# Attention, soft mixture of experts and a dense layer pair in one kernel: a first round over half as many inner columns

## The chip, the core and the metric

The kernel runs on one core of a Trainium2 chip. The metric is the device time of one execution in microseconds (us); the median of three executions of the kernel before is 362.86 us (362.67 to 363.0). Engines are named as in the profile: PE is TensorE (matmul), PEld its weight loads, DVE is VectorE, ACT is ScalarE, POOL is GpSimd, SP is SyncE, which here only issues DMAs.

## The reference

Three parts, one feeding the next. 2304 tokens of width 512 come out of a windowed causal attention (4 batches, 8 heads, 576 positions, head size 64, window 64). A soft mixture of 8 experts with 4 slots each follows, and then the dense layers:

```python
scores = np.where(mask, scale * q @ k.T, -1e9)
x = softmax(scores) @ v                      # -> [2304, 512]
logits = x @ phi                             # 32 slots
slot_in = softmax(logits, axis=0).T @ x      # [32, 512]
slot_out[e] = np.maximum(slot_in[e] @ w1[e], 0) @ w2[e]   # 512 -> 1024 -> 512
x = softmax(logits, axis=1) @ slot_out       # combine, [2304, 512]
h = x @ w_in                                 # 512 -> 2048
out = (h * sigmoid(1.702 * h)) @ w_out       # 2048 -> 512
```

w_in and w_out arrive in float64; the kernel reads them as pairs of 32-bit words and narrows them to float32 itself.

## The kernel before

**Attention and routing.** 18 units of work (16 pairs of heads and two of left-over positions) go through a software pipeline; SP loads q, k and v of the units to come and, in the places given by `W_AT`, one or more blocks of the experts' weights of 1 MB each (`load_w`, 16 of w1 and 16 of w2). The first things that SP loads besides are five raw float64 blocks of 512 KB (`early_load`): four of w_in (128 rows each, inner columns 0 to 511) and one of w_out, into three slots of the weight pool (`raws`). Within the units `convert` narrows each of them over five units, in steps begun at the units in `CONV_AT`: one pass on ACT (L158), one on POOL (L161), three on DVE (L168, L172, L176).

**The experts.** `emit_w1` (L792) multiplies the 32 slots with w1, `emit_w2` (L834, then L893 and L901 for the last two blocks) with w2; four products run side by side on 32 columns of the array each. The w2 blocks come in the order in which they are used; the last one comes in three pieces. Behind the weights SP loads w_out blocks 1 to 4 and w_in blocks 4 and 5, still raw.

**Into the dense layers.** The combine with the slots and w_in are joined: M = slot_out @ w_in, 32 rows, is computed first, and h of a token is its 32 combine weights (`cT`) times M. The columns of M are made in pieces, `MCUT`. Piece 0 (128 columns) is made directly by `emit_m2(0)` (L943). The others go through `emit_m1` (L928, four products side by side, one for each 128 rows of w_in, then a copy to SBUF on ACT, L921) and `emit_m2` (L940, which adds the four up), with the rounded high part written by ACT (L948) and the low part by DVE (L951). Pieces 0 and 1 (columns 0 to 511) are made before the dense loop, the others within it.

**The dense loop.** `steps` is a list of 48 triples (group of inner blocks, round of 768 tokens, inner block of 128 columns). For each step `emit_h` makes h of the next step (L1014), ACT applies the gelu twice (L1002: once rounded, once whole) and DVE takes the difference (`emit_gl`, L1027); `emit_o` then adds the products with w_out's high and low part (L1046) for six tiles of 128 tokens, 18 matmuls in all, into six banks of PSUM, which are all of the accumulators there are. At the last inner block of a group the six are written to SBUF (L1069 on DVE, L1071 on ACT, for later groups an add on DVE, L1066). The order before is four groups of four blocks, and in each the three rounds. Between steps, lists written by hand say at which step a raw block of w_in (`more`) or w_out (`todo`) is narrowed (`conv_a` on ACT, L958; `conv_b` on DVE, four passes, L964, L168, L172, L176), when w_out is split in two (`out_w` on ACT, L982; `out_c` on DVE, L985), and when a further piece of M is made (`mid1`, `mid2`). Each engine takes its instructions in the order in which the program emits them. h, `emit_m1` and `emit_m2` in the loop share two PSUM banks.

Of the kernel before, what the change touches and what calls it, by code (L numbers as in the profile page):

```python
# [38 lines left out]

CONV_AT = {i: n for n, i in enumerate((3, 5, 7, 9, 11))}  # L40
W = (2, 1)
# [24 lines left out]

FP = 4

@with_exitstack
def attention_softmoe_ffn(  # L70
# [113 lines left out]
    def early_dst(n):  # L184
        return win_dst(n) if n < FP else wof[:, n - FP, :]

# [3 lines left out]
    def early_load(n):  # L190
        src = w_in[n] if n < FP else w_out[n - FP]
        if wide:
            raw_load(early_raw(n), src)
        else:
            nc.sync.dma_start(out=early_dst(n), in_=src)
# [397 lines left out]
    nc.sync.dma_start(out=phis, in_=phi.rearrange("p (k s) -> p k s", k=KD))  # L593
    raws = [wslot() for _ in range(3)]
    for n in range(2):
# [17 lines left out]
    for i in range(ns):  # L613
# [53 lines left out]
        if i < 2:  # L667
            for n in range(2 * i + 2, min(2 * i + 4, FP + N_WO)):
                early_load(n)
# [201 lines left out]
    def win_more():  # L871
        n = FP + len(iraw)
        if n == NF:
            return
        if n % FP == 0:
            winf.append(gp.tile([128, 4, 512], F32, tag="wi", name="wi", bufs=2))
        iraw[n] = gp.tile([128, 1024], F32, tag="iraw", name="iraw", bufs=2)
        if wide:
            raw_load(iraw[n], w_in[n])
        else:  # L880
            nc.sync.dma_start(out=win_dst(n), in_=w_in[n])
# [32 lines left out]

    MCUT = [0, 128, 512, 1024, 1536, DFF]
    msb = {}
    mcp = rawt[:, NE * 260:NE * 260 + 512]

# [5 lines left out]
    def emit_m1(j, tag, copy=True):  # L924
        a, w = MCUT[j], MCUT[j + 1] - MCUT[j]
        pm = bank(tag)[:, 0:w]
        for kk in range(KD):
            nc.tensor.matmul(  # L928
                pm[32 * kk:32 * kk + 32, :], soT[:, kk, 0:32],
                win_dst(4 * (a // 512) + kk)[:, a % 512:a % 512 + w],  # L930
                start=True, stop=True, tile_position=(0, 32 * kk))
        msb[j] = mcp[:, a % 512:a % 512 + w], pm
        if copy:
            m1_copy(j)

    def emit_m2(j, tag):
        a, w = MCUT[j], MCUT[j + 1] - MCUT[j]
        pm = bank(tag)[:, 0:w]
        if j:
            nc.tensor.matmul(pm, i4m, msb.pop(j), start=True, stop=True)  # L940
        else:
            for kk in range(KD):
                nc.tensor.matmul(  # L943
                    pm, soT[:, kk, :], win_dst(kk)[:, 0:w], start=(kk == 0), stop=(kk == KD - 1))
        o = mst[:, a:a + w]

        def hi():
            nc.scalar.copy(o, pm)  # L948

        def lo():  # L950
            nc.vector.tensor_tensor(  # L951
                out=o[64:128], in0=pm[64:128], in1=o[64:128].bitcast(F32), op=ALU.subtract)
        return hi, lo
# [37 lines left out]
    NR = NT // ROUND  # L991
    steps = [(p, r, FP * p + k) for p in range(NF // FP) for r in range(NR) for k in range(FP)]
    gs = {}
# [37 lines left out]
    def emit_o(n, between):  # L1031
        p, r, f = steps[n]
        first, last = f % FP == 0, f % FP == FP - 1
        g2 = gs.pop(n)
# [47 lines left out]
    for i in range(14):  # L1082
# [7 lines left out]
        if i == 6:  # L1090
            dctx.close()
            gp = ctx.enter_context(tc.tile_pool(name="gp", bufs=4))
            parts_for(0)
            for _ in range(4):
                wout_load()
            for _ in range(2):
                win_more()
        for f in ahead.get(i, ()):
            f()
# [23 lines left out]
    out_c(1)  # L1123
    out_a(2)
    out_b(2, (0, 1))


    todo = {}
    more, mid1, mid2 = {}, {}, {}
    for p, (at, bt, ms) in enumerate((  # L1130
# [3 lines left out]
        for k in range(FP):  # L1134
            more[at[k]] = FP * (p + 1) + k
            todo[bt[k]] = FP * (p + 1) + k
        mid1[ms[0]], mid2[ms[1]] = p + 2, p + 2
    low = None
    for n in range(len(steps)):
# [7 lines left out]
        if n in todo:  # L1147
            out_b(todo[n])
        if n == 1:
            out_b(3, (0, 1))  # L1150
        between = {}
        if n:
            emit_h(n + 1)
# [4 lines left out]
        if n in mid2:  # L1158
            def second():
                for f in emit_m2(mid2[n], "m"):  # L1160
                    f()
            between.setdefault(2, []).append(second)
        emit_o(n, between)
        if n < 2:
            out_b(n + 2, (2, 3))
        if n in todo or n < 2:
            low = todo.get(n, n + 2)
            out_w(low)
        if n == 0:
            out_a(3)  # L1170
        if n + 1 in more:
            conv_a(iraw[more[n + 1]], win_dst(more[n + 1]))
        if n + 1 in todo and n + 1 > 0 and todo[n + 1] not in wfs:
            out_a(todo[n + 1])
# [5 lines left out]
def _layout(q, k, v, moe_phi, moe_w1, moe_w2, moe2_w_in, moe2_w_out):  # L1180
# [25 lines left out]
    w2 = np.concatenate([w2[:15], last])  # L1206
    wi = moe2_w_in.reshape(4, 128, 4, 512).transpose(2, 0, 1, 3).reshape(16, 128, 512)
    wo = moe2_w_out.reshape(16, 128, 512)
    return {"qk": qk, "vt": vt, "sq": sq, "phi": ph, "w1": w1, "w2": w2,
# [25 lines left out]
```

## Time and profile before

| what | value |
|---|---|
| median of three executions | 362.86 us |
| the profiled execution | 362.31 us, its span 360.5 us |
| granted TensorE clock, mean | 1.000 |
| PE busy | 351.4 us (97%) |
| DVE, ACT busy | 240.5 us (67%), 195.6 us (54%) |
| DMA | 70.87 MB, mean 197 GB/s |

The span runs from the first to the last instruction of the program; 1.8 us of the execution lie around it. PE's 97% is over the whole span, in which DMA is at its limit for the first third and idle for most of the rest, so shares of the whole say little about one stage. Ends of matmuls are modelled.

### The profile page before, as it was taken

Reading aid. Unit: us, or ns where it says so; the run is one execution under the profiler, and the core shown is the slowest. Engines: PE = TensorE matmul, PEld = TensorE weight load, DVE = VectorE, ACT = ScalarE, POOL = GpSimd, SP = SyncE. Lnnn points to the kernel's source line nnn. Section 1 sums busy time; section 2 is a strip of 40 time slices with the busy share of each in tenths; the row PEclk is TensorE's granted clock in tenths of the full one; section 3 lists DMA queues with packets and bytes.
Section 4 is the critical chain, followed back from the end, with each engine's and each line's share of the span. In section 5 each row is a group of like instructions: output and inputs, shape, how many; then the busy total and the mean of one; then the engine's idle time right before and its main releaser. Section 6 shows DMA issues by size and latency. Waiting matters only on the chain.

```text
span 360.5 us, 7741 instructions
## 1 busy us (share of the span) xinstructions
PE 351.4 (97%) x3021; PEld 269.9 (75%) x3021; DVE 240.5 (67%) x527; ACT 195.6 (54%) x499; POOL 45.5 (13%) x90
## 2 busy tenths in 40 slices
PE   7999999998999999999999999999999999999995
PEld 6787787776634357888788887788886888888884
DVE  4666797976626228885867695988687876262624
ACT  2898899777314026765657444554455453333330
POOL 4366764630100000000000000000000000000000
PEclk9999999999999999999999999999999999999999
DMA  7999999999999994233131313140300000040404
GB/s 278 407 414 405 409 407 413 402 404 407 418 418 422 418 402 150 101 121 113 60 116 58 119 57 119 32 137 9 116 2 0 0 2 1 0 176 0 175 2 175
DMA packets 18180, 70.87 MB, mean 197 GB/s; under 512 B 2016, under 2 KB 2400, under 8 KB 14176
## 3 DMA queue, kind: packets, MB, share of 16 engines
q1 hardware_dynamic: 18000, 70.18, 50.3%
q8 instruction: 24, 0.39, 0.4%
q10 hardware_dynamic: 144, 0.20, 0.2%
q14 instruction: 12, 0.10, 0.1%
HBM read 65.65 MB, written 4.72 MB: 195 GB/s over the span
## 4 chain that ended last, share of the span: by engine, by line
PE 86%; DMA 9%; ACT 2%; issue 1%; DVE 1%; DVEq 0%; ACTq 0%
PE s L1046 18%; PE t L1046 18%; PE v L1046 18%; DMA w<-in_w_dram 8%; PE v L363 5%; PE m L1014 5%; PE m L348 5%; PE s L328 4%; PE s L313 2%; PE m L401 2%; ACT pa L340 2%; PE m L442 1%; PE m L492 1%; DMA rawt<-in_qk_dram 1%; PE m L928 1%
## 5 line engine op out<-in xcount | busy, mean ns | idle before, releaser
L1002 ACT ACTIVATE r<-m 128x384 fp32r<-128x384 f32 (+1 forms) x97 | 47.4, 491 | 80.6 <-PE m L1014 80.5
L1027 DVE TENSOR_TENSOR r<-g,r 128x384 fp32r<-128x384 f32 x96 | 51.4, 554 | 48.4 <-ACT g L1002 40.0
L1046 PE MATMUL t<-w,r 128*128 128x512 f32 x288 | 75.8, 395 | 0.0
L1046 PE MATMUL s<-w,r 128*128 128x512 f32 x288 | 74.3, 392 | 0.0
L1046 PE MATMUL v<-w,r 128*128 128x512 f32 (+2 forms) x291 | 73.4, 387 | 0.0
L1046 PEld LDWEIGHTS t<-w,r 128*128 128x128 f32 x288 | 53.8, 188 | 14.8 <-issue 4.0
L1046 PEld LDWEIGHTS v<-w,r 128*128 128x128 f32 x291 | 54.5, 188 | 11.3
L1046 PEld LDWEIGHTS s<-w,r 128*128 128x128 f32 x288 | 52.6, 188 | 8.5
L1002 ACT ACTIVATE g<-m 128x384 f32<-128x384 f32 x96 | 47.8, 499 | 0.0
L340 ACT ACTIVATE pa<-s,nm 128x128 f32<-128x128 f32 x140 | 41.0, 404 | 5.6 <-DVE nm L333 5.6
L333 DVE TENSOR_REDUCE nm<-s 128x4 f32<-128x512 f32 x35 | 22.5, 684 | 5.5 <-PE s L328 4.8
L1014 PE MATMUL m<-cT,w 128*128 128x384 f32 (+2 forms) x113 | 25.9, 320 | 0.0
L1014 PEld LDWEIGHTS m<-cT,w 128*128 128x128 f32 x113 | 20.8, 188 | 4.9 <-ACT g L1002 0.7
L348 PE MATMUL m<-ident,pa 128*128 128x128 f32 x144 | 20.9, 283 | 0.8 <-ACT pa L340 0.4
L348 PEld LDWEIGHTS m<-ident,pa 128*128 128x128 f32 x144 | 15.6, 140 | 5.0 <-PE s L328 1.7
L349 ACT COPY pa<-m 128x512 f32<-128x512 f32 x18 | 10.7, 596 | 10.2 <-PE m L348 10.2
L982 ACT CAST w<-wf 128x512 fp32r<-128x512 f32 x15 | 9.3, 623 | 9.3 <-DVE wf L176 9.3
L792 PE MATMUL s<-w,phis 128*32 128x512 f32 x128 | 14.1, 594 | 0.0
L382 DVE TENSOR_TENSOR arena<-v,rs 128x256 f32<-128x256 f32 x36 | 13.6, 420 | 0.6
L328 PE MATMUL s<-arena 64*64 64x128 f32 x352 | 13.8, 271 | 0.1
L985 DVE TENSOR_TENSOR w<-wf,w 128x512 fp32r<-128x512 f32 x15 | 10.3, 689 | 5.2 <-ACT w L982 4.9
L1066 DVE TENSOR_TENSOR w<-s,w 128x512 f32<-128x512 f32 x18 | 11.6, 684 | 2.8 <-PE s L1046 2.8
(218 smaller groups left out, 453.3 us busy)
## 6 DMA issues: line engine op xcount, KB each, us to landing
w<-in_w_dram SPq DMA_DIRECT2D x24, 1024.0 KB, 9.9
w<-in_w_out_dram SPq DMA_DIRECT2D x16, 512.0 KB, 3.4
arena<-in_w_dram SPq DMA_DIRECT2D x7, 1024.0 KB, 11.4
iraw<-in_w_in_dram SPq DMA_DIRECT2D x12, 512.0 KB, 3.3
arena<-in_qk_dram SPq DMA_DIRECT2D x10, 512.0 KB, 8.8
out_dram<-w SPq DMA_DIRECT2D x16, 256.0 KB, 2.1
arena<-in_vt_dram SPq DMA_DIRECT2D x13, 258.5 KB, 7.3
rawt<-in_qk_dram SPq DMA_DIRECT2D x6, 512.0 KB, 8.7
```

What stands on the lines that cost most here:

```text
L328: nc.tensor.matmul(st[h][rows[j], c, :], q, k, start=False, stop=(c == 3), tile_position=(64 * h, 64 * j))
L333: nc.vector.tensor_reduce(out=nm[:, h], in_=st[h], axis=AX.X, op=ALU.max, negate=True)
L340: nc.scalar.activation(out=pb[h][:, c, :], in_=st[h][:, c, :], func=ACTF.Exp, bias=nm[:, h, c:c + 1], scale=1.0)
L348: nc.tensor.transpose(tt[:, c, :], pb[h][:, c, :], ident)
L363: nc.tensor.matmul(pvt[i][h][64 * j:64 * j + 64, c, :], ab[h][:, c, 64 * j:64 * j + 64], v, start=True, stop=True, tile_position=(0, 64 * j))
L382: nc.vector.tensor_tensor(out=o, in0=pv[h][:, :, 1 - h:65 - h], in1=rs[:, h].unsqueeze(2).to_broadcast([128, 4, 64]), op=ALU.mult)
L792: nc.tensor.matmul(ph[32 * j:32 * j + 32, :], siT[:, kk, :], w1t[4 * r + kk][:, j, :], start=(kk == 0), stop=(kk == KD - 1), tile_position ...
L1002: nc.scalar.activation(out=(gh, g)[part][:, a:e], in_=ph[:, a:e], func=ACTF.Gelu_apprx_sigmoid)
L1014: nc.tensor.matmul(ph[:, c - a:e - a], mst[:, f * 128:f * 128 + 128], cT(c, e - c), start=True, stop=True)
L1027: nc.vector.tensor_tensor(out=gl, in0=g, in1=gh.bitcast(F32), op=ALU.subtract)
L1046: nc.tensor.matmul(accs[t][:, h], a[:, c], b[:, h], start=(first and k == 0), stop=(last and k == 2 and h.stop == 512))
L1066: nc.vector.tensor_tensor(out=o[:, h], in0=accs[t][:, h], in1=o[:, h], op=ALU.add)
```

## The change

Only two blocks of w_in are loaded early, and the host lays the first 512 columns out anew: blocks 0 and 1 now hold all 512 rows of columns 0 to 255, blocks 2 and 3 those of columns 256 to 511. Blocks 2 and 3 are loaded behind the experts' weights and behind w_out block 1, ahead of w_out 2 to 4, and are narrowed in steps 0 and 1 of the dense loop. Piece 1 of M shrinks from 384 to 128 columns; a new piece 2 (256 columns) is made within step 2. The first round of 768 tokens first goes through inner blocks 0 and 1 alone, and takes blocks 2 and 3 together with blocks 4 to 7 when the other two rounds have done blocks 0 to 3; so there are still 12 groups and 48 steps, and the first group ends at step 1, the next ones at steps 5 and 9 (before: 3, 7 and 11). w_out blocks 2 and 3 are narrowed for steps 4 and 5, w_in blocks 4 to 7 one step later than before. h of step 4 is emitted between the tiles of step 3.

```diff
-CONV_AT = {i: n for n, i in enumerate((3, 5, 7, 9, 11))}
+CONV_AT = {i: n for n, i in enumerate((3, 5, 7))}
 FP = 4
+E_IN = 2
     def early_dst(n):
-        return win_dst(n) if n < FP else wof[:, n - FP, :]
+        return win_dst(n) if n < E_IN else wof[:, n - E_IN, :]
     def early_load(n):
-        src = w_in[n] if n < FP else w_out[n - FP]
+        src = w_in[n] if n < E_IN else w_out[n - E_IN]
-    raws = [wslot() for _ in range(3)]
+    raws = [wslot() for _ in range(2)]
-            for n in range(2 * i + 2, min(2 * i + 4, FP + N_WO)):
+            for n in range(2 * i + 2, min(2 * i + 4, E_IN + N_WO)):
     def win_more():
-        n = FP + len(iraw)
+        n = E_IN + len(iraw)
-    MCUT = [0, 128, 512, 1024, 1536, DFF]
+    MCUT = [0, 128, 256, 512, 1024, 1536, DFF]
+    def win_of(a, w, kk):
+        if a < 512:
+            k = 256 * (kk % 2) + a % 256
+            return win_dst(2 * (a // 256) + kk // 2)[:, k:k + w]
+        return win_dst(4 * (a // 512) + kk)[:, a % 512:a % 512 + w]
     # emit_m1, emit_m2: win_of(a, w, kk) in place of win_dst(...)
-    steps = [(p, r, FP * p + k) for p in range(NF // FP) for r in range(NR) for k in range(FP)]
+    groups = [(r, range(0, FP if r else 2)) for r in range(NR)]
+    groups += [(r, range(FP * p + (0 if r or p > 1 else 2 - FP), FP * p + FP))
+               for p in range(1, NF // FP) for r in range(NR)]
+    steps = [(g, r, f) for g, (r, fs) in enumerate(groups) for f in fs]
     def emit_o(n, between):
-        p, r, f = steps[n]
-        first, last = f % FP == 0, f % FP == FP - 1
+        g, r, f = steps[n]
+        p = g // NR
+        first, last = f == groups[g][1][0], f == groups[g][1][-1]
     # behind emit_w2(6)
-            for _ in range(4):
-                wout_load()
+            wout_load()
             for _ in range(2):
                 win_more()
+            for _ in range(3):
+                wout_load()
     # ahead of the loop
-    out_a(2)
-    out_b(2, (0, 1))
-    todo = {}
-    more, mid1, mid2 = {}, {}, {}
+    conv_a(iraw[E_IN], win_dst(E_IN))
+    todo = {2: 2, 3: 3}
+    more, mid1, mid2 = {}, {2: 2}, {2: 2}
-            ((3, 4, 5, 6), (8, 9, 10, 12), (8, 9)),
+            ((4, 5, 6, 7), (8, 9, 10, 12), (8, 9)),
-        mid1[ms[0]], mid2[ms[1]] = p + 2, p + 2
+        mid1[ms[0]], mid2[ms[1]] = p + 3, p + 3
     # in the loop over n
+        between = {}
         if n == 1:
-            out_b(3, (0, 1))
-        between = {}
-        if n:
+            between[2] = [lambda: conv_b(iraw[E_IN + 1], win_dst(E_IN + 1), (0, 1))]
+        if n == 3:
+            between[1] = [lambda: emit_h(n + 1), lambda: emit_gl(n + 1, 0)]
+            between[3] = [lambda: emit_gl(n + 1, 1)]
+        elif n:
             emit_h(n + 1)
-            between.setdefault(2, []).append(second)
+            between.setdefault(2 if n > 2 else 5, []).append(second)
         emit_o(n, between)
-        if n < 2:
-            out_b(n + 2, (2, 3))
-        if n in todo or n < 2:
-            low = todo.get(n, n + 2)
+        if n in todo:
+            low = todo[n]
             out_w(low)
         if n == 0:
-            out_a(3)
+            conv_b(iraw[E_IN], win_dst(E_IN))
+            win_more()
+            conv_a(iraw[E_IN + 1], win_dst(E_IN + 1))
+        if n == 1:
+            conv_b(iraw[E_IN + 1], win_dst(E_IN + 1), (2, 3))
+            win_more()
-        if n + 1 in todo and n + 1 > 0 and todo[n + 1] not in wfs:
+        if n + 1 in todo:
             out_a(todo[n + 1])
     # on the host
     wi = moe2_w_in.reshape(4, 128, 4, 512).transpose(2, 0, 1, 3).reshape(16, 128, 512)
+    first = wi[0:4].reshape(2, 2, 128, 2, 256).transpose(3, 0, 2, 1, 4).reshape(4, 128, 512)
+    wi = np.concatenate([first, wi[4:]])
```

## Rows read from the trace of the kernel before

**Rows 1.** The page's slices, 40 of 9 us each.

```profile
DMA  7999999999999994233131313140300000040404
GB/s 278 407 414 405 409 407 413 402 404 407 418 418 422 418 402 150 101 121 113 60 116 58 119 57 119 32 137 9 116 2 0 0 2 1 0 176 0 175 2 175
```

**Rows 2.** The chain of waits, 88 to 142 us: start, us, what.

```profile
115.71 15.08 DMA w<-in_w_dram
```

**Rows 3.** Timeline of PE, the w2 products: start, us, instruction.

```profile
122.75 6.19 PE L834 MATMUL v<-w,rawt 128*32 128x512 f32 x56
```

**Rows 4.** Timeline of all engines around the last w2 block; in brackets idle time before, releaser.

```profile
130.18 0.16 PEld L901 LDWEIGHTS m<-w,rawt 128*32 128x32 f32 x8 [0.42 <-DMA w<-in_w_dram]
130.38 0.62 DVE L904 TENSOR_TENSOR acc<-m,acc 128x256 f32<-128x256 f32 x2 [10.39 <-PE m L901]
130.84 0.16 PEld L901 LDWEIGHTS v<-w,rawt 128*32 128x32 f32 x8 [0.50 <-DMA w<-in_w_dram]
...
131.19 0.74 PEld L909 LDWEIGHTS t<-i,acc 128*128 128x128 f32 x6 [0.20 <-DVE acc L904]
```

**Rows 5.** The same timeline, up to the first outputs.

```profile
133.50 0.85 PE L928 MATMUL v<-wi,rawt 128*32 128x384 f32 x8
...
134.28 0.67 PE L1014 MATMUL m<-cT,w 128*128 128x128 f32 x3
...
135.00 0.30 PEld L940 LDWEIGHTS v<-rawt,i 128*128 128x128 f32 x2 [0.31 <-ACT rawt L921]
135.00 0.91 PE L940 MATMUL v<-rawt,i 128*128 128x384 f32 x2
...
135.46 1.39 PE L1046 MATMUL s<-w,r 128*128 128x512 f32 x4
```

**Rows 6.** Timeline of PE, starts of steps 1, 2, 8 to 11; L928 of step 8.

```profile
140.87 1.53 PE L1046 MATMUL s<-w,r 128*128 128x512 f32 x6
...
145.53 1.53 PE L1046 MATMUL s<-w,r 128*128 128x512 f32 x6
...
172.29 1.53 PE L1046 MATMUL s<-w,r 128*128 128x512 f32 x6
...
174.44 1.07 PE L928 MATMUL m<-wi,rawt 128*32 128x512 f32 x8
...
178.01 1.53 PE L1046 MATMUL s<-w,r 128*128 128x512 f32 x6
...
183.38 1.53 PE L1046 MATMUL s<-w,r 128*128 128x512 f32 x6
...
187.81 1.54 PE L1046 MATMUL s<-w,r 128*128 128x512 f32 x6
```

**Rows 7.** Line 158, the conversions' ScalarE pass: ns min, median, max.

```profile
L158 ACT ACTIVATE wi<-w x4: 757/760/767, 21.2 to 48.8; 128x512 f32<-128x512 f32 x4
```

**Rows 8.** Timeline of ACT behind step 0.

```profile
142.49 0.62 ACT L982 CAST w<-wf 128x512 fp32r<-128x512 f32 x1 [1.95 <-DVE wf L176]
```

**Rows 9.** The chain of waits, 66 to 92 us.

```profile
75.31 1.33 PE v L363 x32
...
79.32 1.08 PE v L363 x32
```

**Rows 10.** Timeline of PEld, 60 to 92 us.

```profile
75.24 0.74 PEld L363 LDWEIGHTS v<-arena,pa 128*64 128x64 f32 x15 [0.84 <-POOL rawt L244]
```

**Rows 11.** Timeline of DVE in steps 0 to 3.

```profile
140.57 0.56 DVE L1027 TENSOR_TENSOR r<-g,r 128x384 fp32r<-128x384 f32 x1 [0.21 <-ACT g L1002]
...
149.90 0.43 DVE L964 TENSOR_SCALAR wi<-wi 128x512 f32<-128x512 f32 x1
...
152.16 0.55 DVE L1027 TENSOR_TENSOR r<-g,r 128x384 fp32r<-128x384 f32 x1
152.75 0.69 DVE L1069 COPY w<-s 128x512 f32<-128x512 f32 x1
153.35 0.55 DVE L1027 TENSOR_TENSOR r<-g,r 128x384 fp32r<-128x384 f32 x1
```

More of the change, by code (lines that the diff above doesn't have):

```diff
@@ L929, in emit_m1 @@
                 pm[32 * kk:32 * kk + 32, :], soT[:, kk, 0:32],
-                win_dst(4 * (a // 512) + kk)[:, a % 512:a % 512 + w],
+                win_of(a, w, kk),
                 start=True, stop=True, tile_position=(0, 32 * kk))
@@ L943, in emit_m2 @@
                 nc.tensor.matmul(
-                    pm, soT[:, kk, :], win_dst(kk)[:, 0:w], start=(kk == 0), stop=(kk == KD - 1))
+                    pm, soT[:, kk, :], win_of(a, w, kk), start=(kk == 0), stop=(kk == KD - 1))
         o = mst[:, a:a + w]
```

## The prediction

> **What bounds the kernel now.** I read the slices first: the DMA engines are full from the start to about slice 15 of 40, that is to some 136 us of 360.5 [rows 1], and nearly empty later. So the first question is whether the experts' stage waits for its bytes. The chain of waits says yes: its link before the dense layers is one long transfer of experts' weights that lands at 130.8 [rows 2]. TensorE's own timeline says: hardly. The row of seven w2 blocks takes 6.19 us, 0.885 a block, and shows no idle time [rows 3]; only the last block waits for its transfer, 0.42 us for its second piece and 0.50 for its third [rows 4]. TensorE and the transfers thus come out at almost the same moment, and the chain shows only the one that was last. Behind it stands a latency-bound stretch of 4 to 5 us (turn the slots, first piece of the product of slots and w_in, first gelu) [rows 4, 5], and then the dense loop, in which TensorE goes from step to step at 4.43 us (183.38 to 187.81) and is the bound [rows 6].
>
> **What is moved.** Two raw blocks of 512 KB leave the front of the queue. In slice 3 (414 GB/s) they are worth 1.049 MB / 414 = 2.53 us [rows 1]. The queue must not run dry on the way for the weights to keep all of that; the slices up to the fifteenth are full, and how much waits in the queue they don't say. I take a lead of 2.5 us for the last weights; term A needs at most 0.9 of it. The moved blocks are then second and third behind them, at 1.28 us each, and have landed by about 130.8 - 2.5 + 3.8 = 132.1, where ScalarE takes them up at 137 or later: hidden. The w_out blocks 2 to 4, moved behind them, land by 136, and step 4 is now the first to need block 2: hidden too. SP's next loads wait for conversions as before. One raw slot less and the new host order of w_in's first columns cost nothing on the chip; the slots that follow shift by one, and each still waits for the same block of w1 or w2.
>
> **The sum, term by term** (minus is a gain).
>
> *A. The last w2 block.* With the lead both waits, 0.92 us together, go. But VectorE adds the first piece only at 130.38, and the turn of the slots waits for that add: two adds take 0.62, so the first is done at about 130.7 instead of 131.19 with its 0.20 wait [rows 4]. The gain is 131.19 less 130.77: **-0.42**; bounds -0.2 (that wait alone) and -0.92.
>
> *B. The first piece.* `emit_m1(1)`, `emit_m2(1)` are 128 columns wide, not 384. Now TensorE finishes the first h at 134.28 + 0.67 = 134.95, then waits for ScalarE's copy of the wide piece (L921) and runs L940 for 0.91 until 135.91, where the first outputs effectively begin [rows 5]. Narrow, the copy is done before h, and a third of L940 remains: 0.96 - 0.30 = **-0.65**. Bounds: -0.3 (the 0.31 wait alone) and -0.96.
>
> *C. ScalarE's wait.* Behind step 0 the cast of w_out 2 kept ScalarE 1.95 us waiting for VectorE's conversion, with the next gelu behind it [rows 8]; step 1 lasted 140.87 to 145.53, 4.66 instead of 4.43 [rows 6]. In the changed order ScalarE has there only a conversion that reads a landed transfer: **-0.23**; bounds 0 and -0.46 (as much again in step 0).
>
> *D. Attention.* Two of five conversions go (each one pass of ScalarE, 0.76 us [rows 7], three of VectorE, one of GpSimd), and loads land up to 2.5 us earlier. The chain of waits runs through TensorE in these units; the one stall in it that this could take is a product with V at 75.31, 1.33 instead of 1.08 us [rows 9], whose weight load waited 0.84 for GpSimd's memset of the loaded V [rows 10]. **-0.25**; bounds 0 and -1.5, both ScalarE passes whole.
>
> *E. The pieces put into step 2.* A second group of 256 columns means eight more records of L928 and two of L940, where TensorE is the bound. The step with a 512-wide L928 takes 178.01 - 172.29 = 5.72, 1.29 over 4.43; that with L940 5.37, 0.94 over it [rows 6]. Half of 0.94 is 0.47. For L928 a width of 384 took 0.85 [rows 5] and 512 took 1.07 [rows 6], 0.22 for each 128 columns, so 256 fewer give 1.29 - 0.44 = 0.85. **+1.32**; bounds 1.1 (half of both) and 1.8 (0.22 off each). Their copies on ScalarE and the subtraction on VectorE hide behind the other tiles' products; step 3 asks for h of block 2 only behind its second tile, some 1.4 us later, and would wait there if that cover were gone.
>
> The Trainium skill, page "FP8 and Floating Point Precision", section "TensorE Precision Notes", has true FP32 make four passes through the array. At the granted full clock, 2.4 GHz, that is an estimate of 0.43 us for 256 columns, 0.85 for the two products, and the sum would come out 0.47 lower. The trace agrees for L940 (0.94 for 512 columns against 0.85), not for L928 amid the outputs (1.29).
>
> *F. The wait that comes in.* Step 2's L928 needs block 3 converted by VectorE, which works in program order. From 140.57, its last gelu difference of step 0, stand ahead: that difference, block 2 (2.26), a difference, an eviction copy, a difference, and block 3 (2.26) with a second copy between its halves. With 0.59 a difference and 0.60 a copy [rows 11] that is 7.5, so 148.05. TensorE is there from its step 1 start at 140.87 a step of 4.43 and the 2.15 that step 8's L928 comes after its start [rows 6] later: 147.45. **+0.6**, and B moves both sides alike, since step 0's last gelu sets both. Bounds 0 and 1.0. Behind this wait stand the other three tiles and all of step 3; VectorE's next work, W_out 2 (2.26) and two differences, ends near 151.5, and step 3's third product wants the first difference near 152.0: it just fits, so nothing more is charged. The evictions move from steps 3, 7, 11 to 1, 5, 9 at the same count; step 9 gives VectorE some 5.8 us of work in a step of 5.4, which the lighter step 10 takes up: 0.
>
> Sum: -0.42 - 0.65 - 0.23 - 0.25 + 1.32 + 0.6 = **+0.37** on the profiled execution's 362.31, so 362.7. That execution lies 0.55 under the median of the timed runs, 362.86; on that footing 363.2.
>
> **The rivals.** 0.2%, 0.73 us, is about what a measurement of this kernel can tell from no change; each rival is set against it.
>
> *R1, slower: VectorE becomes the bound from step 1 to step 3.* If the evictions and conversions in its queue run 0.6 us later than worked out, step 2 waits 1.2 instead of 0.6, and the half microsecond to spare in front of step 3 is used up, so the wait is paid on once more for W_out 2: 0.4. Sum +1.4, 364.2. For it: seven and a half microseconds of VectorE work against 6.5 of TensorE. Against it: none of the eight operations waits for TensorE. It decides from about 0.4 us on.
>
> *R2, faster: ScalarE paces attention.* If the units in which the two conversions stood waited for ScalarE, its two passes come off the path: D is -1.5 instead of -0.25, the sum -0.88, and on the median's footing 362.0. For it: ScalarE is asked for two copies and eight exponentials in every unit, and TensorE takes turns with it. Against it: the chain of waits there goes from one TensorE line to the next. It decides from D = -1.35 on; if also F were 0, from -0.75 on.
>
> *R3, faster: the lead passes whole.* If the w2 products wait for their blocks all along, and their even pace is that of the transfers (2.53 us for two blocks of 512 KB, that is one of 1 MB, against 0.885 of TensorE: no), A is -2.5 and the sum -1.7: 361.2. The pace of [rows 3] speaks against it; only the chain of waits [rows 2] for it.
>
> *That it does nothing at all* cannot be: E is work added where TensorE is the bound; a time within 0.2% is a balance of terms.
>
> **How the numbers follow.** Forecast (balance, 362.2 to 363.6): 0.43. R1: 0.27, R2: 0.24, R3: 0.06. So faster 0.30, same 0.43, slower 0.27. The range leaves out R3 and the far halves of the bounds in R1, 0.06 and about 0.1: 361.7 to 364.3; the likeliest case alone 362.2 to 363.6.
>
> **What would show it.** The last weights land near 128.3 and L901 has no wait on DMA (A); the first L1046 starts near 134.1 (135.46 [rows 5] less A, B and D) and not below 133.5 (R3); step 1 takes 4.43 (C); between the third and fourth tile of step 2 stands an L928 of eight records behind a wait for L176, near 0.6 us (F; R1 if over 1.1); steps 1 to 4 together are 1.9 us longer than four plain ones (E, F). The forecast is wrong if the first w1 product (L792) starts over 0.8 us earlier, or if steps 3 or 4 wait for VectorE.

## The result, and the profile after

The changed kernel takes 365.24 us, the median of 17 runs from 363.9 to 368.16, against 362.91 for the kernel before beside it (17 runs, 362.3 to 365.26). The ratio is 1.0056 with a 95% interval from 1.0032 to 1.008: slower by 2.3 us, outside the range of the prediction. Medians here are over all runs; ratios and their intervals leave out the few that the chip's slower state disturbed. Single runs lie much further apart than the three shown of before, and not of this kernel alone: in the series of e1 below the kernel before itself ran from 362.18 to 368.35. The profiled execution is one of the longest, 368.16 us (span 366.4), 5.85 more than the profiled one of before, so the trace shows the loss enlarged.

The page's slices of the changed kernel, to be held against [rows 1]:

```profile
DMA  8999999799999995333413304031300000040404
GB/s 290 404 378 406 406 405 405 267 350 379 423 396 421 416 406 191 114 124 113 166 59 114 116 1 172 1 116 57 116 0 0 0 2 1 0 152 22 171 4 172
```

From slice 2 to 15 the kernel before moved 402 to 422 GB/s; here slices 8 to 10 fall to 267, 350 and 379 (and slice 3 to 378). In 70 to 90 us the rate is 310 GB/s against 407: 97 GB/s over 20 us is 1.94 MB not moved, or 4.7 us at 410, more than the 2.5 us that the two removed loads were to give.

The chain of waits of the changed kernel, 50 to 142 us (start, us, what), shows what TensorE did then; [rows 2] and [rows 9] are of the same view:

```profile
54.27 0.26 PE v L364 x2
54.53 1.34 issue
55.86 1.15 PE v L364 x30
...
67.83 0.43 PE s L329 x15
68.26 2.65 issue
70.91 0.76 PE s L329 x17
...
91.72 0.63 PE v L364 x16
92.35 1.70 issue
94.06 0.69 PE v L364 x15
...
106.58 14.28 DMA w<-in_w_dram
...
120.88 15.12 DMA w<-in_w_dram
```

"Issue" is time in which the engine waits for nothing that the profile shows. These pieces stand in the midst of a group of like products: L329 runs 15 of 32, stops for 2.65 us, and runs the other 17, with nothing new to read. The first product of the experts (L793) begins at 103.74, where L792 began at 99.51: 4.23 us late. Timelines of PE, the kernel before and then the changed one:

```profile
99.51 7.07 PE L792 MATMUL s<-w,phis 128*32 128x512 f32 x64
...
132.41 1.16 PE L943 MATMUL s<-wi,rawt 128*128 128x128 f32 x8
```

```profile
103.74 7.07 PE L793 MATMUL s<-w,phis 128*32 128x512 f32 x64
```

The timeline around the last w2 block and the first outputs (start, us, engine, instruction; idle before, releaser in brackets), to be held against [rows 3 to 5]:

```profile
126.98 6.19 PE L835 MATMUL v<-w,rawt 128*32 128x512 f32 x56
...
134.69 0.16 PEld L902 LDWEIGHTS m<-w,rawt 128*32 128x32 f32 x8 [0.38 <-DMA w<-in_w_dram]
135.36 0.16 PEld L902 LDWEIGHTS m<-w,rawt 128*32 128x32 f32 x8 [0.52 <-DMA w<-in_w_dram]
136.04 0.16 PEld L902 LDWEIGHTS v<-w,rawt 128*32 128x32 f32 x8 [0.52 <-DMA w<-in_w_dram]
...
137.62 1.16 PE L951 MATMUL s<-wi,rawt 128*128 128x128 f32 x8
...
139.46 0.67 PE L1025 MATMUL m<-cT,w 128*128 128x128 f32 x3 [0.33 <-DVE w L959]
...
139.97 0.38 PE L948 MATMUL v<-rawt,i 128*128 128x128 f32 x2
...
140.32 1.20 PE L1058 MATMUL s<-w,r 128*128 128x512 f32 x4
```

With 1 MB less ahead of them the last weights still come late: all three pieces of the last block wait for their transfer (0.38, 0.52, 0.52), where two did before. From the first w1 product to the direct piece of M (L951, before L943) it takes 33.88 us instead of 32.90, so the experts lose 0.98 us more behind the 4.23. After that things go as forecast: the second piece is done 140.35 - 137.62 = 2.73 us after the direct piece (L951) began, where before it was 3.50.

The steps of the dense loop, timeline of PE ([rows 6]):

```profile
145.53 1.53 PE L1058 MATMUL s<-w,r 128*128 128x512 f32 x6
...
149.96 1.54 PE L1058 MATMUL s<-w,r 128*128 128x512 f32 x6
...
152.11 0.98 PE L936 MATMUL m<-wi,rawt 128*32 128x256 f32 x8
...
155.45 1.72 PE L1058 MATMUL s<-w,r 128*128 128x512 f32 x6
...
160.44 1.54 PE L1058 MATMUL s<-w,r 128*128 128x512 f32 x6
...
164.94 1.53 PE L1058 MATMUL s<-w,r 128*128 128x512 f32 x6
```

Steps 1 to 4 take 4.43, 5.49, 4.99 and 4.50 us. From the first product of the direct piece to the start of TensorE's last product the changed kernel needs 224.75 us and the kernel before 223.92. This difference, 0.83, is the same within 0.05 in every profiled execution of every kernel below that has the whole change. The dense part therefore costs 0.8 of the 2.3 us, and the rest is lost before it, in the attention and the experts.

**Where the gaps stand.** The page lists a DMA queue of kind "instruction" (q8) with 24 packets and 0.39 MB, 16 KB a packet. The changed kernel has 6,172 records of PE (3,031 products, as many weight loads, 110 waits and the like of its sequencer): 257 a packet. Counting all these records from the start, I listed the longer gaps between one weight load and the next in the attention. Those at which PE waits for data stand at the same records in both kernels. The others stand 256 records, or a multiple of it, apart (to within one):

```
gap of PE (us, from weight load to weight load) before the record with this number; over 0.3 only
record               961   1217   1985   2497   3009   3266     sum
kernel before       0.35   0.63     -    0.50   0.56   1.40    3.44
changed kernel        -    0.51   1.61   3.02   0.83   1.95    7.92
```

The packet that brings the block begun at record 2497 started 6.2 us after PE began the block ahead of it in the changed kernel, and 3.5 us in the kernel before; where no block comes late (e13 below), PE uses up a block in 5.5 to 7.9 us of attention. At each of the ten gaps of the table PE goes on 2.3 to 2.6 us after the start of its packet, which itself takes 0.9 to 1.2: so it is the packet that PE waits for. The Trainium skill, page "Runtime: NRT & Kernel Launch", section "Instruction fetch mechanics", says that a sequencer fetches the next 16 KiB block, 256 instructions, through its own DMA queue while it executes the current one, and that the cost of crossing a block's boundary is mostly hidden. The packets and the spacing of the gaps agree; a gap of 3.02 us does not agree with "mostly hidden", and the measurement decides.

### The profile page after: what moved, and what is told of

Same layout as the page of the kernel before. It is cut to its first block, busy times and chain, and to the rows that moved or that the text cites. A ratio compares the mean times of both kernels' runs of the same rounds, so it can differ in the third digit from the quotient of the medians.

```text
span 366.4 us, 7769 instructions
## 1 busy us (share of the span) xinstructions
PE 351.8 (96%) x3031; PEld 270.0 (74%) x3031; DVE 241.6 (66%) x530; ACT 195.7 (53%) x501; POOL 39.6 (11%) x88
## 4 chain that ended last, share of the span: by engine, by line
PE 84%; DMA 9%; ACT 2%; issue 2%; DVE 1%; DVEq 0%; ACTq 0%
PE s L1058 18%; PE t L1058 18%; PE v L1058 18%; DMA w<-in_w_dram 8%; PE v L364 5%; PE m L1025 5%; PE m L349 5%; PE s L329 4%; PE m L402 2%; PE s L314 2%; ACT pa L341 1%; PE m L443 1%; PE m L493 1%; PE m L936 1%; DMA rawt<-in_qk_dram 1%
## 5 line engine op out<-in xcount | busy, mean ns | idle before, releaser
L1038 DVE TENSOR_TENSOR r<-g,r 128x384 fp32r<-128x384 f32 x96 | 51.7, 554 | 46.5 <-ACT g L1013 41.5
L329 PE MATMUL s<-arena 64*64 64x128 f32 x352 | 13.9, 271 | 2.6 <-issue 2.6
L793 PE MATMUL s<-w,phis 128*32 128x512 f32 x128 | 14.1, 594 | 0.0
L329 PEld LDWEIGHTS s<-arena 64*64 64x64 f32 x352 | 11.4, 133 | 3.5 <-issue 2.9
L373 DVE TENSOR_SCALAR rs<-v 128x4 f32<-128x4 f32 x36 | 5.3, 159 | 12.9 <-PE v L364 12.7
```

The source lines that it names most:

```text
L329: nc.tensor.matmul(st[h][rows[j], c, :], q, k, start=False, stop=(c == 3), tile_position=(64 * h, 64 * j))
L793: nc.tensor.matmul(ph[32 * j:32 * j + 32, :], siT[:, kk, :], w1t[4 * r + kk][:, j, :], start=(kk == 0), stop=(kk == KD - 1), tile_position ...
L1038: nc.vector.tensor_tensor(out=gl, in0=g, in1=gh.bitcast(F32), op=ALU.subtract)
```

## The experiments

Theories: **P**, TensorE's instruction blocks come late in the attention because their fetch waits among the data transfers, and the change only shifted the one against the other. **Q**, the removed loads were a reserve of 1 MB in the queue, and without it the transfers run dry whenever TensorE is held up, since SP issues in order and waits for TensorE's buffers. **D**, the loss is in the dense loop (not the term D of the prediction, which is the attention). Rivals of single runs are in their expectations.

### The early half alone (e1)

```diff
-CONV_AT = {i: n for n, i in enumerate((3, 5, 7, 9, 11))}
+CONV_AT = {i: n for n, i in enumerate((3, 5, 7))}
-    raws = [wslot() for _ in range(3)]
+    raws = [wslot() for _ in range(2)]
-        return winf[n // 4][:, n % 4, :]
+        return winf[n // 4][:, n % (4 if n >= FP else 2), :]
 # and 2 in place of FP where the early blocks are loaded
```

> The kernel before with the early half of the change alone: blocks 2 and 3 of w_in are neither loaded nor converted, and the dense layers read blocks 0 and 1 in their place (that part of the input is left out); the dense loop keeps its old order. Theory P (pages: the attention of the changed kernel loses time because PE's own instruction blocks, fetched through the same 16 DMA engines, arrive after PE has run out of instructions; the removal of two loads only shifts the queue into a worse order): the first product of the experts' w1 starts 1.5 to 4 us later than before's 99.5, with gaps in PE that the chain of waits calls issue, and the time is 364.0 to 365.5. Rival D (the loss is in the dense loop, its two extra pieces and the late conversions): the attention ends at 99.5 or earlier, and the time is 361.5 to 362.9.

364.17 us (12 runs, 362.57 to 369.31) against 363.29; ratio 1.0019, from 0.9978 to 1.006: undecided by the time. In the profile w1 begins at 100.85, 1.34 late, between the two forecasts, and from L943 on it needs what the kernel before needs (223.89). Up to the w1 products this kernel issues the same instructions and loads as the changed one, which began w1 at 103.74. So the early part is not one time but a spread of some us from run to run, and a start of w1 read from one profiled execution, here and below, is one draw of it.

### Two loads put back that nothing reads (e2), or weights in their place (e3)

```diff
 # e2, against the changed kernel (a third raw slot, not shown)
-            for n in range(2 * i + 2, min(2 * i + 4, E_IN + N_WO)):
-                early_load(n)
+            if i == 0:
+                for k in range(2):
+                    raw_load(raws[1].rearrange("p a f -> p (a f)")[:, 1024 * k:1024 * k + 1024], w_in[k])
+            else:
+                early_load(2)
 # e3, against the changed kernel
-W_AT = {**{i: 1 for i in range(2, 17)}, 12: 0, 15: 2, 16: 2, 17: 3}
+W_AT = {**{i: 1 for i in range(1, 17)}, 12: 0, 15: 2, 16: 2, 17: 2}
```

> The changed kernel with two loads of 512 KB put back at their old places, into a third raw slot that nothing reads; the two conversions stay away, and blocks 2 and 3 are loaded late as in the change. Theory P: the queue is that of the kernel before, so the attention is too; w1 starts within 0.6 us of 99.5, and what is left is the dense loop's own loss of 0.7 us: 363.2 to 364.0. Rival D: the time stays within 0.4 us of the changed kernel's (365.2).

> The changed kernel with one block of the experts' weights (1 MB) loaded one unit earlier, in the place of the two loads that the change took away, and one fewer at unit 17. Theory P: the queue's bytes in the attention are those of the kernel before, w1 starts within 0.6 us of 99.5, the last weights land some 2.5 us earlier than before, and the time is 362.6 to 363.4 (before plus 0.7 of the dense loop, less 0.4 for the wait on the last weights). Rival D: 364.8 to 365.6, as the changed kernel. A third outcome, that any order of the queue may do it, would show gaps at other pages and a time between.

363.87 us (ratio 1.0009, 0.9971 to 1.0048) and 363.99 us (1.0011, 0.9977 to 1.0046). In e2 w1 begins at 99.43, with every window from 10 to 128 us at 407 GB/s or more: in the profiled execution 1 MB of useless transfers gave the attention back, and what is left is about the dense loop's 0.8. The time lies in P's range. In e3 w1 begins at 100.46, later than P's limit, and the time lies 0.6 over its range: its gaps at block boundaries sum up to 4.0 us, against 3.44 in the kernel before and 2.85 in e2. The first w1 product in the timelines of PE of e1, e2 and e3:

```profile
100.85 5.36 PE L792 MATMUL s<-w,phis 128*32 128x512 f32 x48
```

```profile
99.43 7.07 PE L797 MATMUL s<-w,phis 128*32 128x512 f32 x64
```

```profile
100.46 5.79 PE L793 MATMUL s<-w,phis 128*32 128x512 f32 x52
```

In e3, at the last w2 block, the timeline of PEld has no wait for a transfer left:

```profile
130.47 0.67 PEld L902 LDWEIGHTS m<-w,rawt 128*32 128x32 f32 x16
...
131.12 0.24 PEld L902 LDWEIGHTS v<-w,rawt 128*32 128x32 f32 x8
131.80 0.74 PEld L910 LDWEIGHTS t<-i,acc 128*128 128x128 f32 x6 [0.45 <-DVE acc L905]
```

From w1 to L951 it takes 32.56 us instead of 32.90, and 32.56 again in e7 and e8, so term A exists and is -0.34 (forecast -0.42). D falls as the cause of more than 0.8; P and Q both stand.

### Half a block further on (e4 to e6)

```diff
+    wv = bank("v")
+    for _ in range(32):
+        nc.tensor.matmul(wv[0:1, 0:1], pa[:, 0:1], pa[:, 0:1], start=True, stop=True)
```

> The changed kernel with 32 one-column products at its start, while TensorE waits for the first loads: the same work, but every later instruction of PE stands half a block of 256 instructions further on. Theory P: the gaps of PE in the attention move to other instructions, by half a block, and the time differs from the changed kernel's by 0.5 us or more, either way. Rival D, and any cause that sits in the data transfers alone: gaps at the same instructions, the time within 0.3 us of 365.2.

> The kernel before with the same 32 one-column products at its start. So far the transfers of the kernel before run at 407 to 418 GB/s in every stretch from 10 to 128 us, those of the changed kernel fell to 310 in 70 to 90. Theory Q (reserve: the two loads taken away were the queue's reserve of 1 MB; without it SP, which issues in order and waits for PE, lets the 16 engines run dry when PE is held up by a late instruction block): the full reserve bears the shift, every stretch stays above 400 GB/s, and the time is within 0.8 us of the kernel before. Theory P alone (the place of the blocks decides): the time moves by 1.5 us or more, as the changed kernel's moved by 2.9.

> The changed kernel with a block of the experts' weights one unit earlier (as in the run weights first), and the 32 one-column products at its start. Theory Q: the reserve of 1 MB is back, so the shift costs little: 363.4 to 364.8, no stretch under 390 GB/s. Theory P alone: 366.5 to 368.5, as the changed kernel with the same shift (368.2).

368.17 (ratio to the kernel before 1.0111, 1.0062 to 1.0159), 366.86 (1.0096, 1.0059 to 1.0133) and 365.61 us (1.0066, 1.004 to 1.0092). The changed kernel (e4) moves by 2.9 us, as P has it. The kernel before (e5), reserve and all, loses 4.0 us, so Q as I put it fails: its rate in 70 to 90 us falls to 351 GB/s too. e6 lies between the two forecasts. But the edit had a fault: its products end at 6.5 us, and the attention starts 1.45 us late. Only the clean shifts below count.

### Two blocks of weights earlier (e7)

`W_AT` as in e3, with 1 at units 0 and 1 and 1 at unit 17.

> The changed kernel with two blocks of the experts' weights (2 MB) issued earlier, at units 0 and 1, and two fewer at unit 17. Theory Q: more reserve than before, all stretches at 400 GB/s or more, 362.8 to 363.8, and the highest of the runs closer to the median than in the run with one block (366.9). Theory P alone: the order of the queue is a new draw, and the time lies anywhere from 363 to 368. A third outcome, that q, k and v now come late behind the weights: TensorE waits for a DMA in the first units, and the time is over 365.

375.83 us (ratio 1.0339, 1.0298 to 1.038): the third outcome, at the other end of the attention. The chain goes from 74.72 us through 7.64 of a load of the left-over positions' q and k, which SP issued late, and from 82.93 through 10.76 of a transfer of weights into the arena, in which the attention has its buffers:

```profile
74.72 7.64 DMA rawt<-in_sq_dram
...
82.93 10.76 DMA arena<-in_w_dram
```

The rate falls to 145 GB/s in 90 to 110 us. Up to 74 us its trace has no gap over 0.3 us at a block's boundary, at 407 to 411 GB/s; whether the larger reserve or the place in the queue did that, one execution can't say.

### Without the two extra products (e8)

```diff
 # against e3
-                    ph[:, c - a:e - a], mst[:, f * 128:f * 128 + 128], cT(c, e - c),
+                    ph[:, c - a:e - a], mst[:, f % FP % (4 - 2 * (f < FP)) * 128 + f // FP * 512:][:, 0:128], cT(c, e - c),
-    more, mid1, mid2 = {}, {2: 2}, {2: 2}
+    more, mid1, mid2 = {}, {}, {}
```

> The run weights first without the two extra products of 256 columns in step 2 (the hidden columns 256 to 512 are not computed; blocks 2 and 3 of the output weights are multiplied with columns 0 to 256 again). It sizes the term of 1.32 us: from the first product of the direct piece to PE's end the kernel before took 223.9 us and all with the change 224.8. As predicted: 223.4 here (1.32 less). If the extra pieces cost nothing and the loss is in waits for conversions: 224.6 or more.

363.38 us (8 runs; ratio to the kernel before 1.0014, 0.9971 to 1.0058). The stretch takes 223.97 us, 0.79 less than with the products, between the two forecasts and not 1.32. The rest of the term comes back as a wait in step 3 for VectorE's gelu difference (L1038), seen in the timelines of PE and PEld:

```profile
149.98 0.61 PE L1058 MATMUL s<-w,r 128*128 128x512 f32 x2
151.11 1.20 PE L1058 MATMUL s<-w,r 128*128 128x512 f32 x4 [0.51 <-DVE r L1038]
...
151.11 0.76 PEld L1058 LDWEIGHTS s<-w,r 128*128 128x128 f32 x4 [0.94 <-DVE r L1038]
```

The products are no pure loss: while TensorE does them, VectorE catches up.

### Clean shifts by a quarter, a half and three quarters (e9 to e12, e15, e16)

One-column products now stand in the place of some of the seven warm-up products and end when those ended (half a block: 36 for four; a quarter: 18 for two; three quarters: 54 for six).

```diff
-    for _ in range(7):
+    wv = bank("v")
+    for _ in range(36):
+        nc.tensor.matmul(wv[0:1, 0:1], pa[:, 0:1], pa[:, 0:1], start=True, stop=True)
+    for _ in range(3):
         nc.tensor.matmul(bank("v")[:, 0:128], pa[:, 0:128], pa[:, 0:128], start=True, stop=True)
```

> The earlier shift by half a block had a fault of its own: its 32 products ended at 6.5 us, and the attention began 1.45 us late (6.54 against 5.09). Here 36 one-column products stand in the place of four of the seven warm-up products, in the same 3.4 us, so that only the place of PE's blocks of 256 instructions moves, by 128. This is the kernel before so shifted. Theory P (place of the blocks decides): the attention begins at 5.1 and the time still moves by 0.8 us or more from 362.9, with gaps at new work. Rival S (it was the late start): 362.4 to 363.4.

> The changed kernel with the same shift by 128 instructions in the same time. Theory P: its distance from the equally shifted kernel before is not the 2.3 us of the unshifted pair; it may be anything from -0.5 to +4. Theory Q (without the two loads the queue has too little in reserve, wherever the blocks stand): it is 1.5 to 3 us slower than the equally shifted kernel before.

> The kernel before shifted by a quarter of a block (64 instructions: 18 one-column products in the place of two warm-up products). Theory P: a third draw, 362.3 to 366. Rival S: 362.4 to 363.4.

> The changed kernel shifted by a quarter of a block. Theory Q: 1.5 to 3 us slower than the kernel before with the same shift; theory P: any distance, and if it is the attention's gaps alone that cost the 2.3 us, there is a shift at which it starts w1 before 100 and ends under 364.

> The kernel before shifted by three quarters of a block (54 one-column products in the place of six warm-up products). It asks whether the kernel before stands at a lucky place. If a shift costs by itself: 366 to 368 as the other two. If the place decides and luck is even: anywhere between 362.5 and 368.

> The changed kernel shifted by three quarters of a block. So far the changed kernel stands to the equally shifted kernel before at +2.3 (no shift), +0.9 (half), -1.2 us (quarter). Theory Q (without the reserve always slower) has fallen already; theory P expects a fourth distance with no rule, within -2 to +4.

Medians, with the ratio to the unshifted kernel before of the same series and its interval:

| shift | kernel before | changed kernel |
|---|---|---|
| none | 362.91 | 365.24; 1.0056 (1.0032 to 1.008) |
| quarter | 367.60; 1.0118 (1.009 to 1.0145) | 366.43; 1.0082 (1.005 to 1.0115) |
| half | 366.08; 1.0071 (1.0044 to 1.0099) | 366.97; 1.0097 (1.0062 to 1.0131) |
| three quarters | 368.98; 1.013 (1.0056 to 1.0205) | 368.31; 1.011 (1.0045 to 1.0175) |

(In the last line's series the unshifted kernel itself ran from 362.45 to 370.58, so only its ratios are to be read.) The attention begins at 5.0 to 5.2 us in all, and moving the blocks by 64, 128 or 192 instructions costs the kernel before 0.7 to 1.3%. e11 (367.60) and e15 (368.98) lie above P's ranges, which end at 366 and 368. The gaps over 0.3 us moved with the blocks in every one of them (records 962, 1474, 1986, 2498 and 3009 among them for e11, at work that stands 64 records earlier), and sum up to between 3.3 and 7.7 us. Shifted alike, the two kernels lie -0.4, +0.3 and -0.2% apart, with intervals of about 0.4, 0.4 and 1% to either side: none can be told from 0, and only the first can be told from the +0.6% without a shift. Q's 1.5 to 3 us appear at none of the three. The kernel before stands at the best of the four places tried; the change, which leaves the blocks of the attention where they are and moves the loads, lost part of that.

e12's expectation asked for a shift at which the changed kernel starts w1 before 100 and ends under 364. In e10 w1 starts at 99.55, but the profiled execution takes 365.45: with 361 GB/s in 70 to 90 us the weights come late, and from w1 to the direct piece it needs 35.28 us instead of 32.90. The loss shows up as a late w1, as late weights, or as both.

A gap may have a second price. In e11 the granted clock of TensorE is 0.50, its level of 1.2 GHz, from 86.5 to 89.9 us, behind the gap at record 3009 (TensorE was busy for 4.49 of 6.40 us from 80 to 86.4); in e12 it is so from 29.9 to 33.3, behind the gap at record 962. The changed kernel's profiled execution kept 1.00 in spite of its gap of 3.02 us. Of its 17 runs five have a mean granted clock of 0.990 to 0.995 and take 366.16 to 368.15 us; the other twelve, at 0.998 or more, have a median of 364.5.

### No weights beside the attention (e13, e14)

```diff
-W_AT = {**{i: 1 for i in range(2, 17)}, 12: 0, 15: 2, 16: 2, 17: 3}
+W_AT = {17: 19}
```

e14 has the quarter shift besides (18 one-column products for two warm-up products).

> The kernel before with all 19 early blocks of the experts' weights issued after the attention (unit 17) instead of beside it: the queue holds only q, k, v and the early raw blocks while the attention runs. The whole is longer by some 40 us, since the experts wait for their weights; what counts is the attention, whose last unit begins at 80.3 us in the kernel before. Theory P in its full form (PE's instruction blocks come late because they stand behind data in the 16 engines): no gap of PE that the chain calls issue over 0.3 us from 10 to 80 us, and the last unit begins by 79.5. Rival B (a block costs its wait by itself, whatever the queue holds): gaps of 0.2 to 1.2 us as before.

> The same, shifted by a quarter of a block (18 one-column products in the place of two warm-up products). With the weights beside the attention this shift delayed its last unit by 6.1 us (86.5 against 80.3). Theory P in its full form: with no weights in the queue the shift is free, and the last unit begins within 0.7 us of that of the run weights late. Rival B, and a rival by which the shift costs time in some other way (banks, clock, the fewer warm-up products): it is later by 3 us or more here too.

394.68 and 395.75 us, one run each; the experts wait for their weights, as they must. The windows from 70 to 90 us, first of the kernel before (start and end, length, busy time and records of PE, PEld, DVE, ACT, POOL, granted clock, DMA share, GB/s):

```profile
70.00:90.00 20.00, 18.59 (x344) 14.51 (x342) 14.65 (x48) 16.32 (x54) 4.96 (x14) 1.00 1.02 407
```

of the changed kernel:

```profile
70.00:90.00 20.00, 18.56 (x343) 14.53 (x343) 13.14 (x42) 14.60 (x47) 2.26 (x9) 1.00 0.83 310
```

of the kernel before shifted by a quarter (e11):

```profile
70.00:90.00 20.00, 17.39 (x306) 13.86 (x306) 14.29 (x44) 12.98 (x44) 4.91 (x14) 0.91 0.88 330
```

and of e13:

```profile
70.00:90.00 20.00, 19.83 (x346) 16.23 (x345) 15.65 (x55) 15.12 (x47) 1.11 (x6) 1.00 0.68 251
```

With the engines at 0.68 instead of 1.02, PE is busy for 19.83 of 20 us. No gap at a block's boundary is left in either run that is longer than the 0.31 us with which PE passes from one line to the next. The sixth to the twelfth packet started 0.2 to 1.9 us after PE began the block ahead of them, against 3.4 to 5.7 in the kernel before. The first score product of the last unit, in the timelines of PE of the kernel before, e11, e13 and e14:

```profile
80.33 0.78 PE L313 MATMUL s<-arena 64*64 64x512 bf16 x4
```

```profile
86.47 0.64 PE L316 MATMUL s<-arena 64*64 64x512 bf16 x4
```

```profile
78.53 0.77 PE L313 MATMUL s<-arena 64*64 64x512 bf16 x4
```

```profile
79.15 0.77 PE L316 MATMUL s<-arena 64*64 64x512 bf16 x4
```

With the weights in the queue the quarter shift costs 6.14 us, without them 0.62, of which 0.56 in the first two units. The clock is not in it either: in e11 it falls only behind this point, in e13 and e14 it is 1.00 up to here. A cost of the shift by itself, of banks or of the warm-up products is thereby excluded: P holds for where the attention loses its time.

## Why the prediction was wrong

The step that failed is **D**, with the sentence on which it rests: "I take a lead of 2.5 us for the last weights", if "the queue must not run dry on the way". I priced the attention by what data it would wait for, and gave it bounds from 0 to -1.5, none of them a loss. Its "issue" pieces I did not ask about: the chain of the kernel before has one of 1.16 us at 88.67. The arrival of TensorE's own instructions it put at nothing. By the runs the part ahead of the dense layers loses 365.24 - 362.91 - 0.83 = 1.5 us in the median, by subtraction. In the profiled execution it loses 4.23 us up to w1, where the gaps at instruction blocks grow from 3.44 to 7.92, and 0.98 in the experts. A gap also holds up SP, whose next loads wait for buffers that TensorE reads: its wait for L329 that spans the gap of 3.02 us is 5.0 us long, and the longest of these three in the kernel before is 2.5. So the rate falls to 310 GB/s and the weights' lead is gone. Without that the forecast's other terms would have brought the time close: e2 and e3 lie 0.6 and 0.7 us above the kernel before of their series. What D did count, the conversions, is not to be seen: in e2, which has the old loads and not the two conversions, w1 begins 0.08 us earlier.

- **A** (-0.42): not to be had in the changed kernel (three waits on the last block instead of two, +0.98 from w1 to the direct piece). Where the weights come in time, in e3, it is -0.34. The 130.77 in its sum stands in no row; with the 130.7 of its own sentence A would have been -0.49.
- **B** (-0.65): the mechanism was right. Step 1 begins 7.91 us after L951 instead of 8.46: -0.55.
- **C** (-0.23): right; step 1 takes 4.43 instead of 4.66.
- **E** (+1.32) and **F** (+0.6): together 1.92 forecast, 1.69 measured (steps 1 to 4 take 19.41, four plain ones 17.72). F was over-sized: VectorE was done with block 3 in time, and L936 waits for it 0.21 us, for its last half only:

```profile
152.11 0.14 PEld L936 LDWEIGHTS m<-wi,rawt 128*32 128x32 f32 x4 [0.35 <-ACT r L1013]
152.47 0.14 PEld L936 LDWEIGHTS m<-wi,rawt 128*32 128x32 f32 x4 [0.21 <-DVE wi L177]
```

  The products took 1.4 gross (steps 2 and 3 are 1.62 longer than plain ones, 0.21 of it that wait), so the rows, 1.32, were nearer than the four-pass estimate, 0.85. Net they cost 0.79, as e8 shows, because they hide a wait for VectorE. Rival R1 saw that VectorE is near its limit; it did not become the bound.
- **The sum** of the dense part, B, C, E and F, was forecast as +1.04 and measured as +0.83.
- **R2 and R3** fell: taking two of ScalarE's passes away moved w1 by 0.08 us in e2, not 1.5, and the seven w2 blocks take 6.19 us in both kernels. The forecast's list of signs did not have what came: for w1 it asked only for a start over 0.8 us earlier, and it began 4.23 later. The resolution of 0.2% was too fine: the three runs of before lay within 0.1%, and with 17 of each kernel the interval is still 0.24% to either side.

What stays open: why a block's packet starts 3.5 us after PE began the block ahead at one place of the queue and over 6 at another. The records do not say on which of the 16 engines a packet ran. Whether a fuller queue helps beside the place (Q) is not settled either: e2 and e3 had the 1 MB back and reached w1 within 1 us of the kernel before, but that is one place, and e7, which should have told, was slow for another reason. How much of the median's 1.5 us is gaps, how much late weights and how much the clock, one profiled execution of each kernel does not tell. No version beat the kernel before: the dense part's +0.83 outweighs A's -0.34 even where the weights come in time.

## What to carry to other kernels

Where thousands of unrolled instructions run beside a saturated DMA queue, the instruction blocks are one of the transfers. Count the engine's records, look for "issue" pieces a constant number of records apart, and keep a range of a per cent open for any edit that moves either stream, even a removal of work. Before a small gain or loss is put down to an edit, time the two kernels at a few shifts of the instruction stream: here a difference of 0.6% at one place was not to be told from none at three others, and at one of these it was clearly another. A load taken out of a queue is worth its bytes only if the queue stays full; the rate by stretch shows whether it did.

## What the runs showed of the hardware that was not expected

- TensorE's instructions arrived as 24 packets of 16 KB. With the data engines at 1.01 to 1.03, a packet started 3.4 to 5.8 us after PE had begun the block ahead of it in the kernel before's attention, from its second packet on, and up to 6.4 in the changed kernel; at 0.55 to 0.68 it was 0.2 to 3.1 us, and the gaps vanished (e13).
- In the stretch with weights alone (105 to 124 us, 417 GB/s in 110 to 128) the packets started only 1.0 to 1.6 us after that point in both kernels, so a full queue by itself does not delay them by 3 us or more.
- 64 PE instructions more at the start, in no more time, moved the whole by 4.7 us (e11).
- Two executions of one and the same attention (the changed kernel and e1) reached w1 2.9 us apart.
- Behind gaps of 2.0 to 2.2 us the granted clock fell to 0.50 for 3.4 us in two profiled executions (e11, e12); behind one of 3.02 us it did not.
